# w_out times phi with phi as the stationary operand in two column strips, and a new layout of the steps

## The chip, the cores and the metric

The kernel runs on one NeuronCore of one Trainium2 chip. The metric is the device time of one execution in microseconds, smaller is better; a version is judged by the median of several executions. The profile is one further execution, recorded by the hardware profiler.

## The reference

Three layers follow one another. The weights w_in and w_out of the second layer come as 64-bit floats and are converted on the chip; the rest is float32.

```python
# 1. recurrent attention, B,H,S,D = 4,8,768,48
for t in range(S):
    cur = einsum('bhd,bhe->bhde', u * kt, vt)
    y[:, :, t] = einsum('bhd,bhde->bhe', rt, state + cur)
    state = wt[..., None] * state + einsum('bhd,bhe->bhde', kt, vt)
# 2. x is y as 3072 tokens x 384; w_in 384x2048, w_out 2048x384
h = x @ w_in
g = h * clip(h + 3, 0, 6) / 6
x = g @ w_out
# 3. soft mixture of experts, phi 384x32 (8 experts x 4 slots)
logits = x @ phi
d = softmax of logits over tokens;  c = softmax of logits over slots
slot_input = d.T @ x
slot_out[e] = relu(slot_input[e] @ w1[e]) @ w2[e]
out = c @ slot_out
```

The kernel never forms x = g @ w_out for all tokens. It forms the product ws = w_out @ phi (2048 x 32) once and takes the logits as g @ ws. The change is in how ws is made.

## The kernel before

The 3072 tokens are 24 groups of 128 (`G`), three of which make one of 8 blocks. Each block has 16 feed-forward steps (`moe_h`, token `h`), one for 128 of the 2048 columns of w_in: nine matmuls on line 498, then a ScalarE activation (L501) and a VectorE operation (L502). 128 such steps are the backbone. Around them, for each group of tokens, lie the loads (`L`, `N`), two VectorE scans (`pw`, `pv`), elementwise products on VectorE or GpSimd (`pk`, `pq`, `rk`, `ru`), the diagonal of the attention matrix on ScalarE or GpSimd (`d0`, `d1`), and the matmuls of attention (`sm`, `kt`, `y`, `tm`). After each four steps `moe_l` (token `l`, L551) adds four slices of ws times g to the logits. At the end stands a tail with the experts.

In the first quarter the weights come in 16 parts: eight of w_in (`W0` to `W7`) and eight of w_out (`V0` to `V7`). A part of w_in is converted from 64 to 32 bits (tokens `A`, `B`: ScalarE L445 and L448, VectorE L458, L460, L462) and split in two (`C`: ScalarE L468, GpSimd L469). Step `h2p` is the first to need part p. A part of w_out is converted in the same way (`a`, `b`), and then `slots_w` (token `c`) makes two of the 16 slices of ws from it.

`slots_w(p)` before: for each of its two slices f it takes a PSUM tile (`rot()`, two such buffers, used by attention as well), turns three 128x128 squares of w_out (L222, by L481), copies the 128x384 result to SBUF on ScalarE (`wt`, L483), runs three fp32 matmuls with the turned square as the stationary operand and 32 columns of phi moving (L485), and copies the 128x32 result to `ws` on ScalarE (L486). An fp32 matmul shows as two weight loads and two passes in the trace.

The order of the work is written by hand. `START` is a list of tokens for the first stretch; then each token has a step of its own by a formula, moved by its entry in `LATER`; `PLACES` gives the order of the 16 weight parts, whose position k sets when a part is converted (step k - 2) and, for w_out, when its `c` comes (two steps later), and the staging buffer that a part shares with others. `RKD`, `RUD`, `PKD`, `PQD` name the groups whose products go to VectorE and not to GpSimd, `DGA` the halves of the diagonal that go to ScalarE. The written order is a priority: the instructions of an engine are placed at compile time by it and by readiness, and each engine then works in the order placed. All DMAs are issued on SyncE's queue.

Of the kernel before, what the change touches and what calls it, by code (L numbers as in the profile page):

```python
# [9 lines left out]
F32 = mybir.dt.float32  # L10
F32R = mybir.dt.float32r
U32 = mybir.dt.uint32
ACTF = mybir.ActivationFunctionType
# [5 lines left out]
DM = H * D  # L19
# [3 lines left out]
NS = NE * SPE  # L23
# [5 lines left out]
KT = DM // 128  # L29
# [135 lines left out]
def emit(ctx, tc, wkr, rkv, u, wi, wo, wot, phi, w1, w2, consts, out, flag=None, ysc=None):  # L165
    nc = tc.nc
# [16 lines left out]
    at = actx.enter_context(tc.tile_pool(name="at", bufs=1))  # L183
# [239 lines left out]
    whl, wof, wsl, stage, cvt = {}, {}, {}, {}, {}  # L423
# [48 lines left out]
    def slots_w(p):  # L472

        r, h = divmod(p, 2)
        cvt.pop(("o", p))
        if h == 0:
            wsl[r] = const.tile([128, 4, NS], F32, name=f"ws{r}")
        for f in range(2):
            ps = rot()
            for kt in range(KT):  # L480
                turn_over(ps[:, kt * 128:(kt + 1) * 128], wof[p][:, f * DM + kt * 128:f * DM + (kt + 1) * 128])  # L481
            wt = at.tile([128, KT, 128], F32, tag="wt", name="wt", bufs=2)
            nc.scalar.activation(out=wt, in_=ps[:, 0:DM].rearrange("p (k c) -> p k c", k=KT), func=ACTF.Copy)  # L483
            for kt in range(KT):
                nc.tensor.matmul(out=ps[:, DM:DM + NS], lhsT=wt[:, kt], rhs=phi_sb[:, kt, :], start=(kt == 0), stop=(kt == KT - 1))  # L485
            nc.scalar.activation(out=wsl[r][:, 2 * h + f, :], in_=ps[:, DM:DM + NS], func=ACTF.Copy)  # L486
# [416 lines left out]
    with ExitStack():  # L903
# [149 lines left out]
        for k, t in enumerate(PLACES):  # L1053
            p = int(t[1:])
            s = k - 2
# [52 lines left out]
RKD = (2, 4, 7, 8, 9, 10, 11, 12, 16, 17, 19, 23)  # L1108
RUD = (4, 10, 12, 18, 20, 21)
PKD = (2, 4, 8, 9, 10, 11, 12, 17)  # L1110
PQD = (0, 2, 3, 7, 10, 11, 19, 20, 23)
LOD = ()
CUT = (0,)
DGA = ((0, 0), (0, 1), (1, 1), (2, 0), (6, 0), (6, 1), (7, 0), (8, 0), (9, 0), (10, 0), (10, 1), (11, 1), (12, 1), (13, 1), (14, 1), (15, 0), (16, 1), (18, 0), (19, 0), (21, 0), (22, 1))
# [19 lines left out]
    'W1': 1, 'W0': 0, 'W3': 3, 'W2': 2, 'W4': 1, 'V0': 4, 'V1': 5, 'W5': 4, 'V2': 2, 'V3': 3, 'V4': 5, 'V5': 4, 'W6': 3, 'V6':  # L1134
# [103 lines left out]
```

## Time and profile before

| what | value |
|---|---|
| time, median of 3 runs | 528.76 us (526.37 to 531.75) |
| profiled execution, own time | 527.37 us |
| its span (first to last instruction) | 525.5 us |
| TensorE busy | 472.2 us (90%) |
| TensorE weight loads busy | 372.6 us (71%) |
| VectorE busy | 366.6 us (70%) |
| ScalarE busy | 242.9 us (46%) |
| GpSimd busy | 147.3 us (28%) |

The span leaves 1.87 us of the profiled time outside it. That execution is 1.39 us faster than the median of the three runs. PE is TensorE's matmuls, PEld its weight loads (they overlap the matmuls), DVE VectorE, ACT ScalarE, POOL GpSimd, SP SyncE. PEclk is TensorE's granted clock as a share of full speed; it has two levels, 1.2 and 2.4 GHz, so a mean of 0.75 says that half of the stretch ran at the lower one.

### The profile page before, as it was taken

How to read it: one execution, taken by the hardware profiler on the slowest of the kernel's cores; microseconds unless marked ns; L12 is line 12 of the kernel's file. 1: busy time of each engine (PE TensorE's matmuls, PEld its weight loads, DVE VectorE, ACT ScalarE, POOL GpSimd, SP SyncE). 2: the span in 40 equal slices, each digit the busy share in tenths (PEclk: the TensorE clock that was granted, in tenths of full speed). 3: DMA queues.
4: the chain of work that ended last, by engine and by line, in shares of the span. 5: the costliest groups of instructions: out<-in, count | busy, mean ns of one | idle time of the engine just before them, and what ended most of it. 6: DMA issues, size and time to landing. Idle time of an engine off the chain costs nothing.

```text
span 525.5 us, 10173 instructions
## 1 busy us (share of the span) xinstructions
PE 472.2 (90%) x3934; PEld 372.6 (71%) x3934; DVE 366.6 (70%) x671; ACT 242.9 (46%) x600; POOL 147.3 (28%) x143
## 2 busy tenths in 40 slices
PE   5766785798999999999999999998999999999992
PEld 5656664687887788886875886777789788753462
DVE  4899999687625577788786789779566667452241
ACT  2574667576664444555353455346224323241021
POOL 4556833425021030323351563344020010000000
PEclk8695898788999999999999999999999999999996
DMA  7974134813113043668848976957597989987957
GB/s 274 416 282 154 60 121 142 327 54 122 62 51 111 1 123 108 185 181 270 273 150 240 325 253 163 318 182 191 153 311 205 386 297 351 416 341 278 405 173 234
DMA packets 40265, 114.14 MB, mean 217 GB/s; under 512 B 4465, under 2 KB 22929, under 8 KB 40209
## 3 DMA queue, kind: packets, MB, share of 16 engines
q1 hardware_dynamic: 40208, 113.41, 63.9%
q8 instruction: 33, 0.54, 0.4%
q14 instruction: 24, 0.19, 0.1%
HBM read 90.34 MB, written 22.02 MB: 214 GB/s over the span
## 4 chain that ended last, share of the span: by engine, by line
PE 54%; DVE 10%; DMA 8%; SPq 2%; ACT 2%; issue 2%; POOL 0%; DVEq 0%; ACTq 0%; POOLq 0%
PE h L498 26%; DMA wkr<-in_wkr_dram 4%; PE rot L222 4%; PE lps L551 3%; PE sides L643 3%; PE sides L306 3%; PE rot L373 2%; PE rot L377 2%; PE rot L799 2%; DMA rkv<-in_rkv_dram 2%; DMA y<-y 1%; PE so L822 1%; DVE e L250 1%; PE po L851 1%; PE rot L485 1%
## 5 line engine op out<-in xcount | busy, mean ns | idle before, releaser
L498 PE MATMUL h<-x,wt 128*128 128x384 f32 x1152 | 232.5, 349 | 16.4 <-DVE g L502 8.4
L498 PEld LDWEIGHTS h<-x,wt 128*128 128x128 f32 x1152 | 201.2, 192 | 37.5 <-DVE g L502 14.3
L501 ACT ACTIVATE g<-h,half 128x384 f32<-128x384 f32 x128 | 72.4, 576 | 65.3 <-PE h L498 55.8
L502 DVE SCALAR_TENSOR_TENSOR g<-g,h 128x384 f32<-128x384 f32 x128 | 68.8, 542 | 39.9 <-ACT g L501 39.2
L529 DVE STREAM_TRANSPOSE gsq<-g 128x384 f32<-128x384 f32 x88 | 49.5, 567 | 3.2 <-DMA via<-gsq 2.0
L250 DVE TENSOR_TENSOR_SCAN e<-wkr,d1r 128x516 f32<-128x516 f32 x24 | 31.2, 1302 | 20.4 <-DMA wkr<-in_wkr_dram 20.3
L295 POOL TENSOR_TENSOR att<-cst,cd 128x512 f32<-128x512 f32 x27 | 33.1, 1234 | 29.3 <-DVE cd L284 27.6
L377 PE MATMUL rot<-att,rkv 128*64 128x128 f32 x384 | 33.1, 298 | 7.1 <-DVE att L311 7.0
L311 DVE COPY_PREDICATED att<-upm,sides 128x512 f32<-128x512 uint32 x48 | 32.5, 723 | 9.6 <-POOL att L295 6.0
L377 PEld LDWEIGHTS rot<-att,rkv 128*64 128x64 f32 x384 | 25.3, 147 | 14.2 <-DVE att L311 8.3
L260 DVE TENSOR_TENSOR_SCAN wkr<-wkr,d1f 128x516 f32<-128x516 f32 x24 | 35.3, 1470 | 0.1
L293 ACT ACTIVATE att<-cst,cd 128x128 f32<-128x128 f32 x84 | 26.6, 393 | 18.5 <-DVE cd L284 18.5
L263 POOL TENSOR_TENSOR wkr<-wkr,e 128x512 f32<-128x512 f32 x16 | 21.9, 1372 | 44.2 <-DVE e L250 33.7
L306 PE MATMUL sides<-wkr 64*128 64x128 f32 x384 | 31.9, 301 | 1.1 <-DVE wkr L270 0.7
L270 POOL TENSOR_TENSOR wkr<-wkr 128x512 f32<-128x512 f32 x15 | 19.8, 1320 | 42.5 <-DVE wkr L260 40.8
L306 PEld LDWEIGHTS sides<-wkr 64*128 64x128 f32 x384 | 26.0, 200 | 7.9 <-issue 4.5
L551 PE MATMUL lps<-g,ws 128*32 128x384 f32 x256 | 29.4, 509 | 0.4 <-DVE g L502 0.4
L349 POOL TENSOR_TENSOR st<-sm,pt 128x192 f32<-128x192 f32 x20 | 12.7, 634 | 55.5 <-DVE sm L348 45.1
L280 POOL TENSOR_TENSOR rkv<-rkv,u_b 128x384 f32<-128x384 f32 x18 | 19.7, 1094 | 26.3 <-DMA rkv<-in_rkv_dram 13.5
L395 ACT ACTIVATE y<-rot 128x384 f32<-128x384 f32 x21 | 10.2, 488 | 35.4 <-DVE y L394 35.4
L267 ACT ACTIVATE wkr<-wkr 128x516 f32<-128x516 f32 x24 | 15.2, 633 | 22.8 <-DVE wkr L270 13.1
L373 PE MATMUL rot<-wkr,st 64*64 64x128 f32 x320 | 24.3, 289 | 1.4 <-ACT ws L486 1.4
(156 smaller groups left out, 654.4 us busy)
## 6 DMA issues: line engine op xcount, KB each, us to landing
piece<-in_w_dram SPq DMA_DIRECT2D x24, 768.0 KB, 8.4
wkr<-in_wkr_dram SPq DMA_DIRECT2D x23, 770.0 KB, 5.4
via<-gsq SPq DMA_DIRECT2D x88, 192.0 KB, 4.2
gnat<-via SPq DMA_DIRECT2D x22, 768.0 KB, 5.9
rkv<-in_rkv_dram SPq DMA_DIRECT2D x24, 640.0 KB, 6.0
wi<-in_wi_dram SPq DMA_DIRECT2D x8, 768.0 KB, 9.1
wo<-in_wo_dram SPq DMA_DIRECT2D x8, 768.0 KB, 4.5
piece<-in_w_dram SPq DMA_DIRECT2D x8, 512.0 KB, 6.6
```

What stands on the lines that cost most here:

```text
L250: nc.vector.tensor_tensor_scan(out=flat(e)[:, ::-1], data0=behind.pop(g)[:, ::-1], data1=flat(d1r)[:, ::-1], initial=0.0, op0=ALU.mult, op ...
L260: nc.vector.tensor_tensor_scan(out=fw, data0=fw, data1=fd, initial=0.0, op0=ALU.mult, op1=ALU.add)
L295: nc.gpsimd.tensor_tensor(out=att[g][:, hs, :], in0=ident.unsqueeze(1).to_broadcast([128, 4, C]), in1=cd[g][:, hs].unsqueeze(2).to_broadca ...
L306: nc.tensor.matmul(out=sps[g][:, x, p * C:(p + 1) * C], lhsT=kt_[hs, p, :], rhs=qt_[hs, p, :])
L311: nc.vector.copy_predicated(out=att[g][:, x::2, :], mask=upm.unsqueeze(1).to_broadcast([128, NP, C]), data=ps[:, x].rearrange("p (a t) -> ...
L373: nc.tensor.matmul(out=ps[hs, k * C:(k + 1) * C], lhsT=stl[g][hs, p, :], rhs=qt_[hs, p, :], start=(k == 0), stop=False)
L377: nc.tensor.matmul(out=ps[64 * x:64 * x + 64, k * C:(k + 1) * C], lhsT=vt[:, 2 * p + x, :], rhs=a[:, 2 * p + x, :], start=(first and k == ...
L498: mm = nc.tensor.matmul(out=ps, lhsT=a[:, wp, f % 2, kt * 128:(kt + 1) * 128], rhs=x_[:, xp, kt, :], start=(kt == 0 and i == 0), stop=(kt ...
L501: ra = nc.scalar.activation(out=t, in_=ps, func=ACTF.Relu, scale=1.0 / 6.0, bias=half)
L502: sv = nc.vector.scalar_tensor_tensor(out=t, in0=t, scalar=1.0, in1=ps, op0=ALU.min, op1=ALU.mult)
L529: nc.vector.transpose(out=gsq[m, q][:, :, :, i, :].rearrange("p r j c -> p j r c"), in_=gt[s].rearrange("p (j r c) -> p j r c", j=n, r=4))
L551: mm = nc.tensor.matmul(out=lps[m][32 * i:32 * i + 32, :], lhsT=wsl[q][:, i, :], rhs=gt.pop(NF * m + 4 * q + i), start=(q == 0), stop=(q = ...
```

## The change

For a part p, `slots_w` now turns both slices first (two PSUM tiles, one `wt` of twice the size in place of two buffers). A third PSUM tile takes the product the other way round: phi is the stationary operand (128x32) and the turned square moves (128 columns). The two slices f go to two strips of 32 output partitions, 64h + 32f, and their matmuls alternate; h is the part's parity. One ScalarE copy brings the 64x128 result to `wsq`. After an odd part, `wsq` holds four slices as 128x128; one more turn on TensorE and one ScalarE copy give the four slices of `ws` as they were before. So `ws` of a pair of parts is written at the second of them.

The steps have new places: 132 tokens get another step, mostly by one or two, and `START` another order. Among them: the conversion of `W5` goes from step 5 to step 7, those of `V2` and `V3` from steps 6 and 7 to 5 and 6, `c2` and `c3` from steps 8 and 9 to 7 and 8; `sm5` goes from 7 to 9; the loads `L8` and `L10` to `L23` mostly come one step later, `L12` four and `L13` three; four groups' products and three halves of diagonals change engines.

```diff
-    whl, wof, wsl, stage, cvt = {}, {}, {}, {}, {}
+    whl, wof, wsl, wsq, stage, cvt = {}, {}, {}, {}, {}, {}
...
             wsl[r] = const.tile([128, 4, NS], F32, name=f"ws{r}")
+            wsq[r] = at.tile([128, 128], F32, tag=f"wq{r % 2}", name="wsq")
+        wt = at.tile([128, 2, KT, 128], F32, tag="wt", name="wt")
         for f in range(2):
             ps = rot()
             for kt in range(KT):
                 turn_over(ps[:, kt * 128:(kt + 1) * 128], wof[p][:, f * DM + kt * 128:f * DM + (kt + 1) * 128])
-            wt = at.tile([128, KT, 128], F32, tag="wt", name="wt", bufs=2)
-            nc.scalar.activation(out=wt, in_=ps[:, 0:DM].rearrange("p (k c) -> p k c", k=KT), func=ACTF.Copy)
-            for kt in range(KT):
-                nc.tensor.matmul(out=ps[:, DM:DM + NS], lhsT=wt[:, kt], rhs=phi_sb[:, kt, :], start=(kt == 0), stop=(kt == KT - 1))
-            nc.scalar.activation(out=wsl[r][:, 2 * h + f, :], in_=ps[:, DM:DM + NS], func=ACTF.Copy)
+            nc.scalar.activation(out=wt[:, f], in_=ps[:, 0:DM].rearrange("p (k c) -> p k c", k=KT), func=ACTF.Copy)
+
+        ps = rot()
+        hs = slice(64 * h, 64 * h + 64)
+        for kt in range(KT):
+            for f in range(2):
+                nc.tensor.matmul(out=ps[64 * h + 32 * f:64 * h + 32 * f + 32, 0:128], lhsT=phi_sb[:, kt, :], rhs=wt[:, f, kt],
+                                 start=(kt == 0), stop=(kt == KT - 1))
+        nc.scalar.activation(out=wsq[r][hs], in_=ps[hs, 0:128], func=ACTF.Copy)
+        if h == 1:
+            ps = rot()
+            turn_over(ps[:, 0:128], wsq.pop(r))
+            nc.scalar.activation(out=wsl[r], in_=ps[:, 0:128].rearrange("p (f s) -> p f s", f=4), func=ACTF.Copy)
...
-RKD = (2, 4, 7, 8, 9, 10, 11, 12, 16, 17, 19, 23)
-RUD = (4, 10, 12, 18, 20, 21)
+RKD = (2, 4, 7, 8, 9, 10, 11, 12, 16, 17, 23)
+RUD = (4, 10, 11, 12, 18, 20, 21)
...
-PQD = (0, 2, 3, 7, 10, 11, 19, 20, 23)
+PQD = (0, 2, 3, 7, 11, 19, 20, 21, 23)
...
-    'W1': 1, 'W0': 0, 'W3': 3, 'W2': 2, 'W4': 1, 'V0': 4, 'V1': 5, 'W5': 4, 'V2': 2, 'V3': 3, 'V4': 5, 'V5': 4, 'W6': 3, 'V6':
+    'W3': 3, 'W1': 1, 'W0': 0, 'W4': 1, 'W2': 2, 'V0': 4, 'V1': 5, 'V2': 2, 'V3': 3, 'W5': 4, 'V4': 5, 'V5': 4, 'W6': 3, 'V6':
...
```

## Rows read from the trace of the kernel before

**Rows 1.** The page: busy time, share and instructions of each engine.

```profile
PE 472.2 (90%) x3934; PEld 372.6 (71%) x3934; DVE 366.6 (70%) x671; ACT 242.9 (46%) x600; POOL 147.3 (28%) x143
```

**Rows 2.** Busy time by stretch: length, PE, PEld, DVE, ACT, POOL, PEclk, DMA.

```profile
20.00:43.00 23.00, 17.07 (x167) 14.16 (x166) 21.52 (x30) 16.70 (x39) 12.03 (x9) 0.80 0.83 304
43.00:60.00 17.00, 11.21 (x59) 9.69 (x59) 17.00 (x17) 5.84 (x14) 13.51 (x9) 0.77 0.36 124
...
75.00:90.00 15.00, 10.20 (x69) 8.10 (x68) 15.00 (x19) 10.61 (x22) 5.01 (x3) 0.89 0.41 142
...
157.00:200.00 43.00, 41.97 (x346) 32.11 (x342) 26.36 (x52) 21.13 (x57) 6.66 (x7) 1.00 0.23 72
...
400.00:463.00 63.00, 63.00 (x402) 52.02 (x401) 41.10 (x96) 23.12 (x48) 2.98 (x10) 1.00 0.95 344
```

**Rows 3.** The same view, in shorter stretches around the slot steps.

```profile
81.00:91.00 10.00, 5.00 (x33) 3.79 (x34) 10.00 (x12) 7.53 (x16) 2.40 (x3) 0.83 0.42 141
...
94.00:99.00 5.00, 3.66 (x33) 3.18 (x33) 2.64 (x3) 2.36 (x6) 2.18 (x2) 0.66 0.98 365
...
102.00:109.00 7.00, 6.81 (x50) 5.09 (x52) 4.76 (x9) 3.51 (x11) 4.24 (x4) 0.51 0.60 210
...
122.00:126.00 4.00, 3.69 (x16) 3.66 (x16) 3.45 (x4) 2.30 (x8) 1.64 (x2) 0.58 0.42 144
126.00:157.00 31.00, 30.72 (x254) 26.46 (x253) 16.05 (x27) 20.22 (x57) 7.65 (x8) 1.00 0.15 48
```

**Rows 4.** Line 485 by itself: weight loads and passes, min/median/max ns.

```profile
L485 PEld LDWEIGHTS rot<-phi_sb,wt x96: 186/192/338, 91.9 to 155.3; 128*128 128x128 f32 x96
L485 PE MATMUL rot<-phi_sb,wt x96: 191/276/402, 92.0 to 155.3; 128*128 128x32 f32 x96
```

**Rows 5.** TensorE's timeline, 100 to 157 us: start, length, line, passes, idle before.

```profile
100.09 0.85 PE L485 MATMUL rot<-phi_sb,wt 128*128 128x32 f32 x6 [0.58 <-ACT wt L483]
...
102.88 1.33 PE L485 MATMUL rot<-phi_sb,wt 128*128 128x32 f32 x6
...
114.67 1.42 PE L485 MATMUL rot<-phi_sb,wt 128*128 128x32 f32 x12
115.93 0.52 PE L222 MATMUL rot<-cst,g 128*128 128x128 f32 x3
...
142.67 1.09 PE L377 MATMUL rot<-att,rkv 128*64 128x128 f32 x16
143.60 0.62 PE L333 MATMUL rot<-rkv,knat 128*64 128x48 f32 x16
```

**Rows 6.** The same view, 176 to 190 us.

```profile
183.42 1.09 PE L377 MATMUL rot<-att,rkv 128*64 128x128 f32 x16
184.44 0.49 PE L306 MATMUL sides<-wkr 64*128 64x128 f32 x2
```

**Rows 7.** Whom TensorE waited for, 90 to 157 us: total us, times, longest.

```profile
PE rot L485 <- ACT wt L483: 1.7, 4, 0.6
PE rot L373 <- ACT ws L486: 1.4, 1, 1.4
...
PE rot L222 <- ACT ws L486: 0.3, 1, 0.3
```

**Rows 8.** ScalarE's copy on line 486, min/median/max ns.

```profile
L486 ACT ACTIVATE ws<-rot x16: 178/198/213, 93.1 to 155.6; 128x32 f32<-128x32 f32 x16
```

**Rows 9.** The page's groups: a 128x128 ScalarE operation, count, busy us, mean ns.

```profile
L293 ACT ACTIVATE att<-cst,cd 128x128 f32<-128x128 f32 x84 | 26.6, 393 | 18.5 <-DVE cd L284 18.5
```

**Rows 10.** TensorE's timeline, 0 to 100 us: step h10.

```profile
84.77 0.79 PE L498 MATMUL h<-x,wt 128*128 128x384 f32 x2 [3.25 <-ACT wt L468]
```

**Rows 11.** VectorE's groups to 160 us: converting w_out, count, busy us, mean ns.

```profile
L462 DVE SCALAR_TENSOR_TENSOR wo<-wo 128x768 uint32<-128x768 uint32 x8 | 9.2, 1150 | 0.1
L460 DVE SCALAR_TENSOR_TENSOR wo<-wo 128x768 uint32<-128x768 uint32 x8 | 9.1, 1151 | 0.1
...
L458 DVE TENSOR_SCALAR wo<-wo 128x768 uint32<-128x768 uint32 x8 | 4.9, 610 | 0.7 <-ACT junk L448 0.7
```

More of the change, by code (lines that the diff above doesn't have):

```diff
@@ L1106 @@
 RB = 2
-RKD = (2, 4, 7, 8, 9, 10, 11, 12, 16, 17, 19, 23)
-RUD = (4, 10, 12, 18, 20, 21)
+RKD = (2, 4, 7, 8, 9, 10, 11, 12, 16, 17, 23)
+RUD = (4, 10, 11, 12, 18, 20, 21)
 PKD = (2, 4, 8, 9, 10, 11, 12, 17)
-PQD = (0, 2, 3, 7, 10, 11, 19, 20, 23)
+PQD = (0, 2, 3, 7, 11, 19, 20, 21, 23)
 LOD = ()
 CUT = (0,)
-DGA = ((0, 0), (0, 1), (1, 1), (2, 0), (6, 0), (6, 1), (7, 0), (8, 0), (9, 0), (10, 0), (10, 1), (11, 1), (12, 1), (13, 1), (14, 1), (15, 0), (16, 1), (18, 0), (19, 0), (21, 0), (22, 1))
+DGA = ((0, 0), (0, 1), (1, 1), (2, 0), (6, 0), (6, 1), (7, 0), (8, 0), (9, 0), (10, 0), (10, 1), (11, 1), (12, 1), (13, 0), (13, 1), (14, 0), (14, 1), (15, 0), (16, 1), (18, 0), (19, 0), (21, 0))
 XP = (2, 4)
@@ L1174 @@
 START = """
-N0 cst L0 msk rk0 L1 N1 wm0 ru0 L2 W0 W1 phi N2 pw0 pk0 W2 pv0 W3 pw1 pc0 pk1 ru1 gp kt0 pv1 d00 pq1 pq0 d10 sm0 sc0 y0 tm0
-rk1 pw2 pc1 tu0 d01 sm1 pv2 yx0 pg0 d11 rk2 pq2 sc1 kt1 pk2 pg2 ru2 pg1 y1 yx1 tm1 pc2 A0 d02 tu1 sm2 B0 A1 d12 kt2 sc2 L3 y2
-B1 tm2 pw3 A2 B2 yx2 N3 C0 C1 pv3 tu2 C2
+N0 cst L0 rk0 L1 N1 msk ru0 L2 W0 W1 phi N2 wm0 pw0 pv0 W3 W2 pw1 pk0 pc0 ru1 pv1 pk1 gp kt0 d00 pq1 pq0 d10 sm0 sc0 y0 rk1
+pw2 tm0 pg0 tu0 sm1 pc1 d01 pv2 d11 yx0 pq2 sc1 kt1 pk2 rk2 pg2 ru2 y1 pg1 sm2 pc2 yx1 tm1 kt2 A0 d02 B0 tu1 A1 d12 sc2 L3 B1
+y2 tm2 pw3 A2 N3 yx2 B2 pv3 C0 C1 tu2 C2
 """.split()
```

62 rows, old and new, of the table LATER are left out of this document.

## The prediction

> **What bounds the kernel now.** I read the page first: TensorE is busy 90% of the span and VectorE 70% [rows 1]. A mean over stages says little, so the second view is busy time by stretch. From 20 to 90 us VectorE is the bound: it is busy 21.52 of 23 us, then 17 of 17, and 15 of the last 15, while TensorE idles 5.8 us of 43 to 60 and 4.8 us of 75 to 90 [rows 2]. From 126 us TensorE is the bound: 30.72 of 31 us, 41.97 of 43, and all of 400 to 463 [rows 2, 3]. Between 90 and 126 us the two meet, and there the slot steps of the 16 parts begin: line 485 runs from 92 to 155 us [rows 4]. What is taken from TensorE there is worth its full length, for all that comes after waits for TensorE; what is taken from it before 90 us is worth nothing unless VectorE feeds it earlier.
>
> The same stretch shows the granted clock as the second thing that matters. It was 0.66 from 94 to 99 us, 0.51 from 102 to 109 and 0.58 from 122 to 126; between and after, 1.00 [rows 3]. At 0.51 almost all of the 7 us is at the lower level, 1.2 GHz. Six passes of line 485 took 0.85 us at the upper level and 1.33 us in that stretch [rows 5]. Idle time of TensorE stands ahead of these falls: 1.4 us until a copy into ws, and 0.58 us until wt [rows 5, 7]. These are waits of the very steps that change.
>
> **TensorE's work.** A part has six matmuls of phi, twelve passes. Today they take 1.26 us from start to the next line's start (114.67 to 115.93) [rows 5]: 0.105 us a pass for only 32 moving columns, so what sets the pace is the 128-column weight load (192 ns each, overlapped) [rows 4]. After the change each load has 32 columns and each pass moves 128, in two strips. The nearest rows are the products of attention on line 377: 128-column passes in two strips of 64. Sixteen take 0.93 us (142.67 to 143.60) [rows 5], 0.116 us for a pair, so the strips run side by side. Six pairs are 0.70 us. The strips also change the array's shape on the way in and out. Where line 377 is followed by another shape, sixteen passes take 1.02 us (183.42 to 184.44) [rows 6], so one change costs 0.09 and two 0.18. A part is then 0.88 us in place of 1.26: 0.38 saved, 3.0 over eight parts. The four new turns cost at most 0.52/3 = 0.17 each [rows 5], 0.7 together. Net: **-2.3 us**. Its bounds: -3.8 if the changes of shape vanish among those that the neighbours make anyway (8 x 0.56 - 0.7), +3.2 if the strips of 32 don't overlap (twelve passes of 0.116 and 0.18, 1.57 us a part). I take the middle since line 377 has the same pattern of passes.
>
> What the shape changes cost is read from the rows above. The Trainium skill (TensorEngine Tiling (Array Packing), section Key Properties) has a rule that speaks against the change: changing the tiling mode, not just the tile, drains TensorE. By the rows that is 16 changes of 0.09, 1.4 us; without such a drain the saving would be 3.7 us and not 2.3.
>
> The same page (section Instruction Overhead) says that each matmul has about 60 cycles of overhead, so that a matmul of one column takes as long as one of 60. As an estimate from it, at 2.4 GHz a pass of line 485 would be 0.025 us and the old block 0.3 us, and the swap would lose 0.58 us a part. The measured 0.105 us a pass is for this same block and is used instead.
>
> **ScalarE and the buffers.** Today a part has two copies of 384 columns and two of 32; after, the same two large ones, one of 64x128, and one of 128x128 for two parts. A 32-column copy takes 0.198 us [rows 8], a 128x128 operation 0.393 [rows 9]. So 0.40 us a part becomes between 0.30 and 0.59, at most 1.5 us over all; ScalarE is busy 20.22 of 31 us there [rows 3], which hides it. If it weren't hidden, it would be those 1.5 us. VectorE and GpSimd get nothing from this part.
>
> **Waits.** Idle time that ends on the slot steps' copies is 1.7 + 1.4 + 0.3 = 3.4 us today [rows 7]. Each of the two slices has its own chain of turn, copy, matmul, copy, and holds one of two PSUM buffers throughout; attention (line 373) and the turns of g queue behind those. Afterwards a buffer is free as soon as its wt is copied, and matmuls wait once a part, not twice: I halve the 3.4 to get -1.7. New is that in every second part the turn of wsq waits for the copy just before it, and behind it on TensorE waits whatever is placed next, a step h or attention; l, which needs ws, waits too. A copy of 0.393 and some 0.2 of latency bound that at 0.6 a time, 2.4 for four; with half of it covered by other passes, +1.2. Sum **-0.5 us**, between -3.4 and +2.4.
>
> **The clock.** The three low stretches cost about half of what ran in them at the lower level: 1.7 us (94 to 99), 3.4 (102 to 109), 1.7 (122 to 126), 6.8 in all [rows 3]. With fewer waits I expect one of the shorter ones to go, **-1.5 us**; bounds -6.8 (all go) and +3.4 (one more like the longest).
>
> **The layout.** The written order is only a priority, so it can't be followed exactly to what each engine runs. What matters is the stretch to 105 us: later moves meet a TensorE that idles 1 us in 43 [rows 2]. There the main move is that the conversion of W5 comes behind those of V2 and V3. Step h10 already waits 3.25 us for W5 [rows 10]. A conversion of w_out takes VectorE (9.2 + 9.1 + 4.9)/8 = 2.9 us [rows 11], so h10 can come up to 5.8 us later. Against that, c2 and c3 can run sooner, in the 5 us that TensorE idles from 81 to 91 [rows 3], which takes them from the later stretch where TensorE is full. Two slot steps are some 1.26 us of products each and their turns, about 3.6 us with six turns each at 0.1. Bounds: -5.0 (that idle filled) and +5.8. The rows give no side clearly; the c steps weigh a little more, since h10 has no one behind it that other passes couldn't replace: **-1.0 us**. The loads of wkr are issued later by one to four steps of some 3 us on SyncE's queue, ahead of products that VectorE starts two or more steps after in the written order for most groups. They cost nothing while TensorE has 1 us of idle in 43; should one come too late, VectorE's slack of 16 us in that stretch covers it, and without that cover each costs its delay, up to 3 us.
>
> The sum is -2.3 - 0.5 - 1.5 - 1.0 = **-5.3 us**. The profiled execution took 527.37 us, 1.39 under the median of the three runs; from the profile the sum gives 522.1 and on the median's scale **523.5 us**, which I predict. One per cent, 5.3 us, is about what a measurement of this kernel can tell from no change, so the forecast lies on that edge.
>
> **Rivals.** First, **more is freed than counted**: with one product block a part, the clock stays up through 94 to 126 (-6.8) and the slot waits go (-3.4), with the work at -2.3: -12.5, 516.3 us. For it: each fall has a slot wait ahead of it. Against: the conversions on VectorE still pace the slot steps.
>
> Second, **the waits are only exchanged**: the work saves 2.3, but the turn's new waits (+2.4 against -1.7) and an unchanged clock leave -1.6, 527.2 us, no change. For it: the written order is made so that TensorE is full only from 126 us, and all of its other idle has other causes, VectorE above all.
>
> Third, **W5 decides**, on the slower side: h10 is placed on TensorE ahead of c0 to c3 and waits for two more conversions, +5.8, and through that longer idle the clock falls for one more stretch like 102 to 109, +3.4; with -2.3 that is +6.9, 535.7 us. It decides from h10 starting 2.3 us later than today, at 87.1 us; from 84.8 + 7.6 = 92.4 us on, or earlier with the fall, the kernel is over 1% slower. Against it: today c0 was written before h10 and placed behind it, so the placement follows readiness.
>
> Fourth, **the strips don't overlap** and the change doesn't do what it says: +3.2 for the work, rest nothing, 532.0 us. Line 377 speaks against it.
>
> Fifth, **the clock falls where it is 1.00 now**. From 126 to 157 us the twelve-pass blocks keep TensorE busy at the upper level, and after the change there are fewer passes and more turns. One stretch like 102 to 109 more costs 3.4, less 2.3 of work: +1.1, 529.9 us. The Trainium skill (TensorE: Matmul & The Clock Gate, Part 4: PE-mode transpose) says that transposes don't count as busy for the clock in the way of matmuls. Against that stands the clock of 1.00 over 31 us with many turns in them [rows 3].
>
> **How the numbers follow.** Forecast 0.36 (its own range 520 to 526, half of it faster by over 1%), more freed 0.26, exchanged 0.22, W5 0.09, no overlap 0.03, the clock's fall 0.04. Faster by over 1%: 0.18 + 0.26 = 0.44; slower by over 1%: 0.09; within: 0.47. The range is 515 to 531: it holds the first, the second, the exchange and the clock's fall with their spread, and leaves out W5, no overlap and the far end of the unknown bounds.
>
> **What would show it.** Right: line 485's successor takes about 0.9 us a part, with pairs of passes a few ns apart and 32-column weight loads; waits on slot copies under 3 us from 90 to 157; fewer stretches at the lower clock before 126 us; the last h step some 5 us earlier than 463. Wrong: passes of the two strips 0.1 us apart; long idle before h10; new low-clock stretches behind the turn of wsq; a step h waiting for a late wkr after 200 us. Above all a shift of the whole early stretch by VectorE's order, which I can't read from the written order, would move the result either way.

## The result and the profile after

The changed kernel takes 532.18 us (median of 17 runs, 530.31 to 535.85), the kernel before 530.45 (17 runs, 525.31 to 533.78). The ratio is 1.0054, with an interval of 1.003 to 1.0078: half a per cent slower, where 523.5 us was predicted. Ratios are formed from the executions in the faster of two states alone, so they need not be the quotient of the medians, here 1.0033. The profiled run of after took 532.18 us, its own median. The profiled run of before [rows 1] lies 3.1 us under the median of these 17, so the two traces together overstate the loss; a second trace of before stands beside them below.

The page of after, busy time of each engine:

```profile
PE 467.5 (88%) x3938; PEld 363.4 (69%) x3938; DVE 366.0 (69%) x671; ACT 243.4 (46%) x600; POOL 148.0 (28%) x142
```

TensorE is busy 4.7 us less than in [rows 1], and the span is 4.9 us longer (530.4): TensorE idles 9.6 us more. Busy time by stretch of after, with the columns of [rows 2], says where:

```profile
90.00:105.00 15.00, 10.29 (x113) 7.25 (x109) 9.91 (x14) 11.50 (x29) 8.32 (x7) 1.00 0.66 232
105.00:120.00 15.00, 12.19 (x85) 9.57 (x87) 8.92 (x16) 9.59 (x23) 4.37 (x3) 0.89 0.32 120
120.00:135.00 15.00, 12.06 (x90) 9.39 (x91) 13.44 (x19) 9.11 (x24) 7.12 (x5) 1.00 0.48 159
135.00:157.00 22.00, 20.80 (x188) 16.79 (x187) 10.60 (x18) 13.51 (x39) 4.35 (x5) 1.00 0.09 32
...
400.00:463.00 63.00, 62.15 (x404) 50.16 (x401) 39.44 (x94) 21.69 (x46) 2.95 (x10) 1.00 0.90 323
```

In the first three of these stretches the granted clock was 0.79, 0.87 and 0.89 before, with the 0.66, 0.51 and 0.58 of [rows 3] inside them; it is now 1.00, 0.89 and 1.00. But from 90 to 157 us TensorE is idle 4.71 + 2.81 + 2.94 + 1.20 = 11.7 us, where before has 5.2 in the same four. And the stretch from 400 us, full before [rows 2], has 0.85 us of idle.

To compare versions I use one stretch, from the start of step 0 of the feed-forward to that of step 24, which holds all slot steps. The row of before and that of after, same columns:

```profile
43.08:162.11 119.03, 101.04 (x749) 85.05 (x749) 91.75 (x125) 74.14 (x185) 47.22 (x35) 0.88 0.36 121
```

```profile
42.97:162.95 119.98, 94.83 (x753) 75.61 (x754) 92.14 (x125) 74.48 (x181) 50.49 (x35) 0.93 0.35 120
```

Idle is length less busy: 18.0 and 25.2 us. Time at the lower clock level is twice the missing share: 2 x 0.12 x 119.03 = 28.6 and 2 x 0.07 x 119.98 = 16.8 us. Half of it is lost where TensorE works; counted so for all of it, idle time too, it is an upper estimate. So +7.2 of idle, -5.9 by the clock, and -0.3 left over for the work itself make the +0.95. (PEclk has two digits: the lower-level time is good to 1.2 us each, so the last two terms are known to about 1 us only.)

Which wait is it? Whom TensorE waited for from 43 to 157 us (total us, times, longest), in before:

```profile
PE h L498 <- DVE g L502: 5.2, 5, 3.0
```

and in after:

```profile
PE h L508 <- DVE g L512: 10.8, 6, 3.3
...
PE rot L222 <- ACT wsq L492: 1.5, 4, 0.4
...
PE rot L490 <- ACT wt L484: 1.0, 3, 0.6
...
PE rot L373 <- ACT ws L496: 0.7, 1, 0.7
PE rot L222 <- ACT wt L484: 0.6, 1, 0.6
...
PE lps L561 <- ACT ws L496: 0.4, 1, 0.4
```

The wait that grew by 5.6 us is not a slot step's own: it is a feed-forward step waiting for VectorE's product of an earlier step. TensorE's timeline of after shows the longest one after 90 us, and what became of the slot products (start, length, line, passes, idle before):

```profile
92.32 0.62 PE L508 MATMUL h<-x,wt 128*128 128x384 f32 x2 [1.58 <-ACT wt L468]
...
103.20 0.55 PE L222 MATMUL rot<-cst,wo 128*128 128x128 f32 x3
106.17 2.12 PE L508 MATMUL h<-x,wt 128*128 128x384 f32 x9 [2.42 <-DVE g L512]
...
111.00 0.84 PE L490 MATMUL rot<-wt,phi_sb 128*32 128x128 f32 x10
111.78 0.55 PE L222 MATMUL rot<-cst,g 128*128 128x128 f32 x3
...
137.29 0.41 PE L490 MATMUL rot<-wt,phi_sb 128*32 128x128 f32 x2
137.66 1.16 PE L306 MATMUL sides<-wkr 64*128 64x128 f32 x16
138.75 0.84 PE L490 MATMUL rot<-wt,phi_sb 128*32 128x128 f32 x10
...
151.77 0.85 PE L490 MATMUL rot<-wt,phi_sb 128*32 128x128 f32 x12
152.55 0.55 PE L222 MATMUL rot<-cst,g 128*128 128x128 f32 x3
```

VectorE's timeline of after for the wait that ends at 106.17:

```profile
101.99 1.55 DVE L458 TENSOR_SCALAR cv<-cv 128x768 uint32<-128x768 uint32 x1
...
103.57 0.96 DVE L460 SCALAR_TENSOR_TENSOR cv<-wi,cv 128x768 uint32<-128x768 uint32 x1
104.45 1.23 DVE L260 TENSOR_TENSOR_SCAN wkr<-wkr,d1f 128x516 f32<-128x516 f32 x1
105.59 0.99 DVE L512 SCALAR_TENSOR_TENSOR g<-g,h 128x384 f32<-128x384 f32 x2
```

TensorE stands still from 103.75 to 106.17 because the product that frees its step (L512, 105.59) comes behind a conversion and a scan in VectorE's order. The slot steps have a smaller part in it: ScalarE's activations ahead of these products began at 102.69, after 0.54 us of waiting for `l0` (L561), ahead of which TensorE had waited 0.39 us for `ws`.

The slot products, line 490 by itself, to compare with [rows 4]:

```profile
L490 PEld LDWEIGHTS rot<-wt,phi_sb x96: 106/110/155, 88.8 to 155.3; 128*32 128x32 f32 x96
L490 PE MATMUL rot<-wt,phi_sb x96: 272/273/419, 88.8 to 155.4; 128*32 128x128 f32 x96
```

A weight load of 32 columns takes 110 ns, not 192. A part in one piece takes 0.78 us from start to the next line's start (151.77 to 152.55), against 1.26 before [rows 5]. But only two of the eight parts run so. In six the first pair of passes goes as soon as the first `wt` is there, and the other ten wait for the second. The pair costs 0.37 (137.29 to 137.66), and the ten cost 0.78 like all twelve (111.00 to 111.78), since one strip still has six passes to do: 1.15 together.

### The profile page after: what moved, and what is told of

Read it like the earlier page. It is cut to its first block, busy times and chain, and to the rows that moved or that the text cites. A ratio compares the mean times of both kernels' runs of the same rounds, so it can differ in the third digit from the quotient of the medians.

```text
span 530.4 us, 10169 instructions
## 1 busy us (share of the span) xinstructions
PE 467.5 (88%) x3938; PEld 363.4 (69%) x3938; DVE 366.0 (69%) x671; ACT 243.4 (46%) x600; POOL 148.0 (28%) x142
## 3 DMA queue, kind: packets, MB, share of 16 engines
q1 hardware_dynamic: 40208, 113.41, 62.9%
## 4 chain that ended last, share of the span: by engine, by line
PE 53%; DVE 20%; DMA 13%; issue 4%; ACT 4%; SPq 3%; POOL 2%; DVEq 0%; POOLq 0%; ACTq 0%
PE h L508 26%; DMA wkr<-in_wkr_dram 6%; PE rot L222 4%; PE sides L653 3%; PE rot L377 3%; PE lps L561 3%; DMA rkv<-in_rkv_dram 3%; DVE wkr L260 3%; DVE e L250 3%; PE rot L373 3%; DMA y<-y 3%; PE sides L306 2%; PE rot L809 2%; SPq L400 2%; DVE cv L460 2%
## 5 line engine op out<-in xcount | busy, mean ns | idle before, releaser
L508 PE MATMUL h<-x,wt 128*128 128x384 f32 x1152 | 236.5, 352 | 22.5 <-DVE g L512 14.2
L512 DVE SCALAR_TENSOR_TENSOR g<-g,h 128x384 f32<-128x384 f32 x128 | 68.6, 541 | 37.0 <-ACT g L511 36.4
L295 POOL TENSOR_TENSOR att<-cst,cd 128x512 f32<-128x512 f32 x26 | 30.7, 1191 | 28.8 <-DVE cd L284 27.0
L293 ACT ACTIVATE att<-cst,cd 128x128 f32<-128x128 f32 x88 | 27.8, 390 | 18.5 <-DVE cd L284 18.5
L349 POOL TENSOR_TENSOR st<-sm,pt 128x192 f32<-128x192 f32 x20 | 14.2, 709 | 55.9 <-DVE sm L348 24.2
L267 ACT ACTIVATE wkr<-wkr 128x516 f32<-128x516 f32 x24 | 15.2, 632 | 31.4 <-DVE wkr L270 16.9
L561 PE MATMUL lps<-g,ws 128*32 128x384 f32 x256 | 28.7, 498 | 0.4 <-ACT ws L496 0.4
L280 POOL TENSOR_TENSOR rkv<-rkv,u_b 128x384 f32<-128x384 f32 x17 | 19.3, 1133 | 16.8 <-DMA rkv<-in_rkv_dram 12.1
L732 POOL COPY c<-chi 128x128 f32<-128x128 f32 x6 | 2.2, 364 | 77.5 <-DVE chi L730 39.7
```

What stands on the lines that cost most here:

```text
L293: nc.scalar.activation(out=att[g][:, h, :], in_=ident, func=ACTF.Copy, scale=cd[g][:, h:h + 1])
L295: nc.gpsimd.tensor_tensor(out=att[g][:, hs, :], in0=ident.unsqueeze(1).to_broadcast([128, 4, C]), in1=cd[g][:, hs].unsqueeze(2).to_broadca ...
L508: mm = nc.tensor.matmul(out=ps, lhsT=a[:, wp, f % 2, kt * 128:(kt + 1) * 128], rhs=x_[:, xp, kt, :], start=(kt == 0 and i == 0), stop=(kt ...
L512: sv = nc.vector.scalar_tensor_tensor(out=t, in0=t, scalar=1.0, in1=ps, op0=ALU.min, op1=ALU.mult)
L561: mm = nc.tensor.matmul(out=lps[m][32 * i:32 * i + 32, :], lhsT=wsl[q][:, i, :], rhs=gt.pop(NF * m + 4 * q + i), start=(q == 0), stop=(q = ...
```

## The experiments

Each ratio is to the kernel before on the same chip, with its 95% interval. The table collects, for the stretch from step 0 to step 24, the length, TensorE's idle time, its time at the lower level worked out as above, and VectorE's busy time; and the length from step 88 to 112 (us).

| version | ratio | steps 0-24 | idle | lower level | VectorE | steps 88-112 |
|---|---|---|---|---|---|---|
| before | 1 | 119.0 | 18.0 | 28.6 | 91.8 | 61.3 |
| before_again | 0.9991 (0.9951 to 1.0032) | 119.1 | 18.1 | 31.0 | 91.7 | 61.3 |
| after | 1.0054 (1.003 to 1.0078) | 120.0 | 25.2 | 16.8 | 92.1 | 62.9 |
| code_alone | 1.0028 (0.9991 to 1.0064) | 122.9 | 22.3 | 32.0 | 93.1 | 61.3 |
| layout_alone | 1.0094 (1.0064 to 1.0123) | 123.6 | 20.2 | 34.6 | 92.4 | 64.3 |
| early_new | 1.0001 (0.9968 to 1.0034) | 120.9 | 23.5 | 24.2 | 93.5 | 61.3 |
| late_new | 1.0071 (1.004 to 1.0102) | 120.9 | 24.9 | 16.9 | 93.0 | 63.3 |
| after_old62 | 0.9999 (0.9962 to 1.0037) | 119.8 | 24.4 | 16.8 | 93.7 | 61.3 |
| few_products | 1.0002 (0.9965 to 1.0038) | 122.1 | 22.8 | 36.6 | 92.9 | 61.3 |
| light_convert | 1.014 (1.0083 to 1.0198) | 125.3 | 23.6 | 35.1 | 81.8 | 61.3 |
| whole_after | 1.0108 (1.0061 to 1.0154) | 123.8 | 29.5 | 22.3 | 92.2 | 63.7 |
| whole_old62 | 1.0076 (1.005 to 1.0102) | 125.0 | 27.2 | 30.0 | 92.8 | 61.7 |

**The two halves of the change.** My first theory was that the slot products are as good as forecast and the layout costs; the rival, that the products themselves bring nothing. code_alone has the new `slots_w` in the old layout, layout_alone the old one in the new layout.

```diff
 # code_alone: only slots_w of the diff; START, PLACES, LATER and the engine lists stay
 # layout_alone: only those; slots_w stays
```

> The new slot products (phi stationary, two strips, the extra turn) with every step where it was before. Theory A (the work saved on TensorE is real, but the stretch to some 157 us is not bound by TensorE, so it comes back as idle time; what was lost came from the layout): TensorE busy falls by 3 to 5 us, the time lies 0 to 2 us under the kernel before (ratio 0.996 to 1.000). Rival B (the new slot steps themselves cost, by the turn that waits for its copy and by ws coming later): 2 to 4 us slower than before (ratio 1.004 to 1.008), most of it lost before step h24. Rival C (the saving is worth its full length): ratio 0.990 to 0.994.

> The old slot products with every step where the change puts it. Theory A: the layout costs, and the slot products save nothing that could offset it: ratio 1.004 to 1.010, so as slow as the whole change or a little slower. Rival B (the slot steps cost): ratio 0.996 to 1.002. Rival C: about 1.010 or more, since the saved work of 2 to 5 us is missing.

The layout by itself costs 0.9%. By the ratios the new products take back 0.4 points of it in their own layout (layout_alone to after), though the two intervals overlap, and they bring nothing in the old one (1.0028, its interval holds 1). TensorE's timeline of code_alone shows one place where the saving goes:

```profile
124.41 0.88 PE L222 MATMUL rot<-cst,wo 128*128 128x128 f32 x6
128.83 4.62 PE L508 MATMUL h<-x,wt 128*128 128x384 f32 x16 [3.55 <-DVE g L512]
```

and that of before the same place:

```profile
127.08 0.55 PE L222 MATMUL rot<-cst,wo 128*128 128x128 f32 x3
127.46 0.75 PE L485 MATMUL rot<-phi_sb,wt 128*128 128x32 f32 x6
128.38 2.53 PE L498 MATMUL h<-x,wt 128*128 128x384 f32 x13 [0.17 <-DVE g L502]
```

In both the step starts at 128.4 to 128.8, when VectorE is through. Before, turns and slot products fill the time until then; afterwards they are done, and TensorE waits.

**The layout cut in two.** early_new has the new `START` and `PLACES` and the moves of tokens up to step 26 (46 tokens), late_new the other 86 moves and the new engines; both have the new products. after_old62 is the whole change with the 45 moves from step 62 on, and the engines of groups 19 to 22, put back.

```diff
-    'N7': -5, ..., 'L12': -2, ..., 'pk20': 2, ...     (before)
+    early_new:   the new value where the token's step is 26 or less, else the old
+    late_new:    the old value there, else the new
+    after_old62: the old value where the token's step is 62 or more, else the new
```

> The new slot products; the new START, PLACES and all moves of tokens up to step 26 (46 tokens), and the old places and engines of all later tokens. If the loss lies in the early stretch (the conversion of W5 behind V2 and V3: h10 came 7.5 us later in the trace after): ratio 1.003 to 1.008, and step h24 at 163 us or later. If it lies in the later steps: ratio 0.996 to 1.001, with the steps from h72 on as early as before.

> The new slot products; the old START, PLACES and early places, and the new places and engines of the 86 tokens moved after step 26. If the loss lies in the later steps: ratio 1.003 to 1.008, with the distance to before growing between h74 and h108 as in the trace after (from 1.4 to 5.0 us). If it lies in the early stretch: ratio 0.996 to 1.001.

> The changed kernel with the 45 tokens from step 62 on, and the engines of groups 19 to 22, put back to their old places. Theory A (what the change loses lies in the later steps, between h64 and h112, where three kernels with the new late places took 141.6 to 144.3 us and three with the old ones 138.9 to 140.7): that stretch takes 138.9 to 140.8 us again and the ratio to before is 0.997 to 1.002. Rival (the loss comes from the places between steps 27 and 61, or from the early ones): the ratio stays at 1.004 to 1.007, whatever that stretch shows.

early_new and after_old62, with the old late steps, end at 1.000; late_new and after, with the new ones, at 1.007 and 1.005. So the new late steps cost about half a per cent; what the early part of the layout costs with the old products was not run by itself. The windows from step 88 to 96, 96 to 104 and 104 to 112 show part of it; before:

```profile
368.59:397.35 28.76, 28.76 (x284) 22.56 (x284) 17.05 (x38) 7.55 (x15) 4.01 (x5) 1.00 0.77 236
397.35:412.27 14.92, 14.92 (x91) 13.17 (x91) 11.84 (x26) 7.05 (x15) 0.00 (x0) 1.00 0.77 237
412.27:429.88 17.61, 17.61 (x117) 13.75 (x117) 9.92 (x24) 4.97 (x10) 0.00 (x0) 1.00 0.95 353
```

and after:

```profile
371.92:398.63 26.71, 26.71 (x252) 20.86 (x252) 16.64 (x38) 7.05 (x14) 4.05 (x5) 1.00 0.76 241
398.63:416.87 18.24, 17.39 (x124) 14.73 (x124) 11.61 (x26) 7.39 (x16) 0.00 (x0) 1.00 0.66 208
416.87:434.85 17.98, 17.98 (x117) 13.62 (x117) 10.26 (x25) 5.09 (x10) 0.00 (x0) 1.00 0.96 351
```

32 passes, those of lines 373 and 377 for the last group, went from the first window to the second. The first gave up 2.05 us for that, the second took 3.32, 0.85 of them idle. Three windows together: 61.29 and 62.93. TensorE's timeline of after has the idle ahead of step 102:

```profile
412.62 1.83 PE L508 MATMUL h<-x,wt 128*128 128x384 f32 x9 [0.85 <-DVE g L512]
```

The last column of the table repeats it: 61.3 in the versions with the old late steps (61.7 in whole_old62), 62.9 to 64.3 in each with the new.

**How much may be saved at all.** few_products runs one of the three products of a slice: 6.7 us of TensorE less. light_convert leaves out two of VectorE's three operations on a part of w_out: 14 us of VectorE less. before_again is the kernel before, traced again.

```diff
 # few_products, in slots_w of before
-            for kt in range(KT):
-                nc.tensor.matmul(..., lhsT=wt[:, kt], rhs=phi_sb[:, kt, :], start=(kt == 0), stop=(kt == KT - 1))
+            nc.tensor.matmul(..., lhsT=wt[:, 0], rhs=phi_sb[:, 0, :], start=True, stop=True)
 # light_convert, in to_f32, for parts of w_out
-        nc.vector.tensor_scalar(...)            # L458
-        nc.vector.scalar_tensor_tensor(...)     # L460
```

> The kernel before, with only one of the three products of a slice (kt = 0): 8 of 12 passes of a part are left out, 0.84 us a part and 6.7 us in all, and the logits miss two thirds of their terms. Theory A (the stretch to some 157 us isn't bound by TensorE): 0 to 2 us faster, ratio 0.996 to 1.000. Rival (TensorE's work there is worth its length, as I predicted): 5 to 7 us faster, ratio 0.987 to 0.991.

> The kernel before, with the first two of VectorE's three operations on each part of w_out left out (1.76 us a part, 14 us in all, about half of it before 94 us), so that the converted w_out has wrong values. Theory A (VectorE sets the early stretch, and TensorE's work there fits into its shadow): 5 to 10 us faster, ratio 0.981 to 0.991, steps h10 to h24 earlier. Rival (TensorE sets it): at most 2 us faster, ratio 0.996 to 1.000.

> The kernel before once more, for a second trace of it. The profiled execution of the first was 3.1 us under the median of its 17 runs. If that was a lucky early stretch (the clock, the order of transfers), this trace has step h24 one to three us later than 162.1, and the same 138.9 us from h64 to h112. If early stretch and later steps are steady, both agree within 0.5 us.

The row of few_products from step 0 to 24:

```profile
42.51:164.59 122.08, 99.27 (x686) 81.27 (x686) 92.87 (x125) 74.70 (x185) 48.23 (x35) 0.85 0.34 118
```

63 passes are gone, and the stretch is 3.05 us longer than in before: idle +4.8, half of 8.0 us more at the lower level +4.0, work -5.8. The time is the same (1.0002). With VectorE 10 us less busy (light_convert) it is even longer, with more idle and lower clock as well. So neither of these two pieces of work, one of TensorE's and one of VectorE's, is worth its length in this order.

This holds even where TensorE was full and the clock at the upper level throughout. From step 16 to step 24, before:

```profile
130.06:162.11 32.05, 31.94 (x279) 27.21 (x278) 15.49 (x27) 20.07 (x56) 4.71 (x5) 1.00 0.22 71
```

and few_products:

```profile
132.68:164.59 31.91, 28.95 (x252) 24.29 (x251) 14.43 (x27) 19.15 (x53) 5.05 (x5) 1.00 0.20 71
```

TensorE has 3.0 us less to do and idles 2.85 us more; the stretch is 0.14 us shorter. Most of the new idle time is one wait, on TensorE's timeline of few_products:

```profile
147.72 4.26 PE L497 MATMUL h<-x,wt 128*128 128x384 f32 x23 [1.82 <-DVE g L501]
```

and VectorE's timeline has a load of wkr in front of it:

```profile
144.05 1.23 DVE L250 TENSOR_TENSOR_SCAN e<-wkr,d1r 128x516 f32<-128x516 f32 x1 [3.34 <-DMA wkr<-in_wkr_dram]
...
147.14 0.99 DVE L501 SCALAR_TENSOR_TENSOR g<-g,h 128x384 f32<-128x384 f32 x2
```

In before the same scan waits 3.27 us for its load:

```profile
140.18 1.23 DVE L250 TENSOR_TENSOR_SCAN e<-wkr,d1r 128x516 f32<-128x516 f32 x1 [3.27 <-DMA wkr<-in_wkr_dram]
...
143.38 1.03 DVE L502 SCALAR_TENSOR_TENSOR g<-g,h 128x384 f32<-128x384 f32 x2
```

and TensorE comes to the same step at 144.15 without idle time. There its other work just filled the wait: TensorE was busy, and still it had no time to give back before the product was there.

**A tie through the logits.** Next theory: steps of the feed-forward fill `NG` = 8 buffers of g, and `l` frees four only when its slices of `ws` are there; so the slot chain sets the stretch through `l`. Rival: the buffers are not what waits. g_ten has ten buffers, and `NTL` (tiles that the tail holds) 8 for 9 to make room; g_eight_control has only the latter, g_seven seven buffers. l0_first makes step 10 wait for `l0`.

```diff
-NG = 8
+NG = 10          # g_seven: 7
-NTL = 9
+NTL = 8          # g_ten and g_eight_control
-PIN = {'L5': 'h1', 'L6': 'h0'}
+PIN = {'L5': 'h1', 'L6': 'h0', 'h10': 'l0'}      # l0_first alone
```

> The kernel before with ten buffers for g in place of eight (NG = 10); to make room, the tail holds one piece of the experts' weights fewer beforehand (NTL = 8), as in its control. Theory D (the early stretch is set by neither engine but by the eight g buffers: the ninth g can't be written until l0 has read the first four, and l0 waits for ws; in ten traces g8 starts 0.5 to 4.5 us after l0, g12 after l1): step h24 comes 2 to 6 us earlier than in its control, ratio to the control 0.988 to 0.996. Rival (the g buffers only seem to bind, TensorE and its clock would be late anyway): 0.997 to 1.003.

> The control for ten buffers: the kernel before with NTL = 8 and eight buffers. It differs in the tail alone, so h24 comes as in before (161.7 to 162.1 us in two traces); the tail may take up to 2 us longer, ratio to before 1.000 to 1.004, by every theory.

> The kernel before with seven buffers for g. Theory D: g7, which starts at 79.1 us today, has to wait for l0 as g8 does (some 105 us), and each later g one step longer: 3 to 8 us slower, ratio 1.006 to 1.015, lost before h24. Rival (not binding): 0.998 to 1.003.

> The kernel before with one more edge: h10 is queued behind l0 on TensorE (today l0 runs at 105.2 us, 20 us behind h10). Theory D: c0, c1 and l0 come earlier since nothing stands between, l0 at 95 to 101 us, and h24 follows by 2 to 4 us: ratio 0.992 to 0.997. Rival (TensorE's work or its clock binds): h10's later start costs what l0 gains, 0.998 to 1.004.

g_ten 1.0293 (1.0241 to 1.0345), g_eight_control 1.0033 (0.9992 to 1.0073), g_seven 1.0482 (1.0435 to 1.0529), l0_first 1.0231 (1.0188 to 1.0274). One buffer less costs, more than the theory's 1.006 to 1.015, and two more cost too, where it said faster: the stretch from step 0 to 24 grows to 123.9 us in g_ten, 131.4 in g_seven and 134.1 in l0_first. More buffers don't free it. (In g_ten the stretch also holds 90 passes fewer than in before, 659 for 749, and step 24 starts 4.6 us later where the whole trace is 21.7 us longer: most of its loss lies behind step 24 and isn't explained here.) The tie itself is there; on ScalarE's timeline of before:

```profile
106.69 1.52 ACT L501 ACTIVATE g<-h,half 128x384 f32<-128x384 f32 x3 [2.25 <-PE lps L551]
```

Then the tie was cut: `l` takes a slice of phi in place of `ws`, the work being the same. With it came the new products (l_free_code), one product of three (l_free_few) and the whole change (l_free_after).

```diff
-            mm = nc.tensor.matmul(out=..., lhsT=wsl[q][:, i, :], rhs=gt.pop(NF * m + 4 * q + i),
+            mm = nc.tensor.matmul(out=..., lhsT=phi_sb[:, 0, :], rhs=gt.pop(NF * m + 4 * q + i),
```

> The kernel before, with a slice of phi in place of ws as the stationary operand of the l steps (the logits are then wrong; ws is still made, but nothing reads it). Theory D (the early stretch is set by the chain of slot steps, l and the g buffers): h24 comes 6 us or more before 162 us, ratio 0.975 to 0.990. Rival (TensorE's work and the clock, or VectorE, set it anyway): h24 within 3 us, ratio 0.994 to 1.003.

> The new slot products with the old layout, and l freed in the same way. Theory D: with the tie cut, the stretch to h24 is set by TensorE's work, so the saving of 2.3 to 4.7 us shows: 2 to 5 us faster than the old products with l freed. Rival: no difference to them beyond 1 us, as there was none with the tie (1.0028).

> The old layout with one of three products of a slice (6.7 us of passes left out) and l freed. Theory D: 4 to 7 us faster than all products with l freed. Rival: no difference, as there was none with the tie (1.0002).

> The whole change with l freed. Theory D together with the loss in the later steps: the same 0.4 to 0.7% slower from h64 on as without the freeing (142 us and more from h64 to h112 against 139), the early stretch as in the new products with the old layout or up to 3 us later, so 2 to 5 us slower than these. Rival: as slow against l freed alone as the change is against before (1.005).

l_free 1.0201 (1.0137 to 1.0266; 540.08 us), l_free_code 1.01 (1.0031 to 1.0169; 534.44), l_free_few 1.0082 (1.0044 to 1.0121; 533.32), l_free_after 1.0102 (1.0025 to 1.0179; 535.01); the medians are of the executions behind the ratios. Taking the tie away makes the kernel 2% slower, so the tie isn't what keeps it from being faster, and the theory falls. But among these versions the saving shows: leaving out two thirds of the products is worth 6.8 us, about its length of 6.7. The new products come to 5.6, though there the intervals overlap. What the same work is worth depended on the order around it.

**The parts in one piece.** Last: was the saving never made, because six of eight parts run in two pieces? With the second slice first, no pass can start before both are there.

```diff
         for kt in range(KT):
-            for f in range(2):
+            for f in (1, 0):
```

> The whole change, with the two slices' matmuls in the other order (f = 1 first). In the trace of the changed kernel six of eight parts run their slot products in two pieces, one pair of passes (0.34 to 0.41 us) as soon as the first wt is there and ten passes (0.77 to 0.84) once the second is; an undivided block takes 0.78. With f = 1 first, the first matmul already needs the second wt, so all twelve passes should run in one piece. First theory, the pieces ate the saving and TensorE's time counts in full: 6 x 0.37 = 2.2 us less, ratio to the kernel before 1.0054 - 0.0042 = 1.001. Second, time saved on TensorE comes back as waits for VectorE or as lower clock, as it did when two thirds of the products were left out: ratio stays at 1.005 (1.002 to 1.008) though the blocks measure 0.78. Third, the new placement disturbs the early stretch: 1.008 or more, with the 24th step later than 165 us.

> The whole change with the old places from step 62 on (0.9999 before), and f = 1 first in the slot products. First theory (the pieces ate the saving): 2 us less, ratio 0.996, which would be faster than both kernels. Second theory (saved time comes back as waits): 0.9999 within 0.003. Third (new placement disturbs the early stretch): 1.004 or more.

All eight parts now take 0.78 to 0.85 us and ten-pass pieces are gone (in whole_old62 one, at the lower clock, takes 1.30). The time didn't get shorter: whole_after is 1.0108 against 1.0054 for the change as it was, with intervals that overlap, and whole_old62 is 1.0076 against 0.9999, clearly longer. In both the third expectation came true; step 24 comes at 167.2 and 167.9 us. TensorE's waits for VectorE's product are now 13.2 us from 43 to 157 us. One chain of it can be followed in whole_after; first TensorE's timeline:

```profile
118.78 1.09 PE L373 MATMUL rot<-wkr,st 64*64 64x128 f32 x16 [0.70 <-ACT ws L496]
...
123.53 0.62 PE L508 MATMUL h<-x,wt 128*128 128x384 f32 x2 [0.90 <-ACT wt L468]
126.96 1.01 PE L508 MATMUL h<-x,wt 128*128 128x384 f32 x2 [2.81 <-DVE g L512]
```

then SyncE's, and VectorE's:

```profile
119.94 0.33 SPq L234 DMA_DIRECT2D wkr<-in_wkr_dram  x1
```

```profile
122.48 0.28 DVE L394 COPY y<-rot 128x128 f32<-128x128 f32 x1
124.74 1.72 DVE L250 TENSOR_TENSOR_SCAN e<-wkr,d1r 128x516 f32<-128x516 f32 x1 [1.98 <-DMA wkr<-in_wkr_dram]
126.38 0.52 DVE L512 SCALAR_TENSOR_TENSOR g<-g,h 128x384 f32<-128x384 f32 x1
```

Attention waits 0.70 us for the PSUM tile that the slot step's last copy held. Line 373 frees a buffer of wkr, whose load is issued 1.2 us after it starts. The scan on VectorE waits for that load until 124.74, 1.98 us, and the product behind it in VectorE's order frees TensorE at 126.96. In after the same chain stands (line 373 at 118.90, load 120.07, scan 124.54), but the wait for the product is 0.85, and a slot block runs behind it at 126.82. Why other versions wait for VectorE at other places isn't settled by one chain.

## Why the prediction was wrong

**The step that failed** stands in the first part: "What is taken from TensorE there is worth its full length, for all that comes after waits for TensorE." In the order of before it was worth nothing: few_products took away 6.7 us of the slot products, half of them between 90 and 126 us and half from 127 to 156, and the time was 1.0002. The reading ahead of it failed too, "From 126 us TensorE is the bound": from step 16 to 24, where TensorE had been busy 31.94 of 32.05 us, 3.0 us less work came back as 2.85 us of idle. At the two places followed above, steps at 128.4 and 144.15 us of before, TensorE was full because slot products or attention lay in a time in which it would have waited for VectorE, and VectorE, ahead of the second, for a load. That this holds in the whole stretch is argued from them and not shown. I had taken busy for setting the pace, and priced the stretch in which VectorE and TensorE meet as TensorE's alone.

**TensorE's work**, -2.3 us: right in kind, wrong in size. An undivided block takes 0.78, less than the forecast 0.88. But six parts came in two pieces at 1.15: 2 x 0.48 + 6 x 0.11 = 1.6 saved, less four turns of 0.17 = 0.7, so -0.9. I had priced the twelve passes as a block and not asked that both copies be there before the first pass. The strips overlap (that rival is out), and beside six pairs at line 377's pace (0.70) the two changes of shape cost 0.78 - 0.70 = 0.08 together, not 0.18. The Trainium skill (TensorEngine Tiling (Array Packing), Key Properties) says that a change of the tiling mode drains TensorE. As far as these rows show it, the drain is small here: the 0.08 for two changes.

**Waits**, -0.5: those of the turn of wsq came to 1.5 us in four, near the 1.2 forecast. That rested on a copy of 0.393 us and 0.2 us of latency; no run shows the 0.2. The copy (L492) took 0.27, and the waits were 0.36 to 0.37 each. The others fell from 3.4 [rows 7] to 1.0 + 0.7 + 0.6 + 0.4 = 2.7. Sum +0.8, inside the bounds.

**The clock**, -1.5: it was more, some -5.9 from step 0 to 24 by the estimate above, near the far bound of -6.8. Rival five (the clock falls from 126 us) is out. But the gain came with 7.2 us of idle: whether TensorE works at the lower clock or at the upper one and waits, the stretch stays 119 to 120 us (before, after, after_old62).

**The layout**, -1.0: the late steps, which I priced at nothing since TensorE idles 1 us in 43, cost half a per cent (early_new 1.0001, after_old62 0.9999, after 1.0054). A TensorE without idle time was no cover: passes moved from one full window to the next left 0.85 us of idle and a longer sum. Early, together with the new products, the layout neither won nor lost. W5 did come late, step 10 at 92.32 against 84.77 [rows 10], far past the point that I gave for the rival. Yet it decided nothing in the changed kernel: step 12 started at 109.42, before 111.20.

**Rival two**, the waits are only exchanged, is nearest to what happened: 527.2 us and no change. Its reason was too small: not the turn's waits took the place, but those for VectorE.

**What stays open.** Each edit also changes the order in which the instructions are placed at compile time. No run here takes work away and keeps the order, so I can't say how much of a loss is the saved work turned into waits and how much is another order. That saving doesn't pay in this stretch in the order of before is shown; what would make it shorter is not. No version was faster than the kernel before, whichever part was edited. That would also fit an order written for the old durations, which any edit disturbs, and no run separates the two.

## What to carry to other kernels

Before work on a busy engine is priced at its length, leave it out in a kernel of its own and time that: it estimates what a faster version can bring in that order, and here it would have said zero in one run. An engine that is full can still be only filling the time until another one. Where code and a written order change together, time them apart; here the products in the old order made no measurable difference and the late order cost half a per cent. And a block that is fast only in one piece needs all its operands before its first pass.

## What was unexpected of the hardware

Ten passes in two strips take as long as twelve (0.77 to 0.84 against 0.78 us), when one strip still has its six: a lone early pair saves nothing and costs 0.37. Undivided, twelve passes of 128 columns with a 32-column load take 0.065 us each, where twelve of 32 columns with a 128-column load take 0.105. And less work came with a lower clock: in the trace with 63 passes less, the time at the lower level from step 0 to 24 was 36.6 us, against 28.6 and 31.0 in two traces of before.
